# An execution order from a table: attention with a shared key head beside a squared-ReLU layer, on one core

## The chip, the cores and the metric

The program runs on one core of a Trainium2 chip. The time is what the device needs for one execution, in microseconds (us). One execution was taken by the hardware profiler; the views quoted below come from it.

## What is computed

The input x has 2048 rows of 640 values in bfloat16. Each row is normalised to mean 0 and variance 1. The normalised rows go through an attention with 32 query heads of 20 values that share one key and one value head, and through a layer with 1536 hidden values whose activation is the square of a ReLU. Both results are added to x.

```python
xn = (x - mean) / sqrt(var + 1e-5)                     # x: 1 x 2048 x 640
q = heads(xn @ wq)                                     # 32 heads of 20
p = softmax(q @ (xn @ wk).T * 20 ** -0.5)              # one key head for all
a = rows(p @ (xn @ wv)) @ wo
h = relu(xn @ w1 + b1)
out = x + a + (h * h) @ w2 + b2
```

## The kernel before, in words

**Blocks and tiles.** The work of the attention is cut into 32 blocks (`NBLK`): 4 parts of 512 query rows, and for each of them 8 groups of 4 heads. A block has 16 key tiles of 128 keys, and a key tile has 4 score tiles, one for each head: 128 keys by 512 queries. There are 2048 score tiles. A score tile is one product on TensorE (`ps<-qT,kT`) with only 20 rows of the array, so up to four heads can run side by side, each in its own quarter of rows. It lands in one of the eight PSUM banks; bank 7 (`PVB`) holds the sums of the block, the other seven hold scores and the results of all other products.

**Two ways to the exponential.** 1392 of the score tiles go to ScalarE, two in one instruction (L1022, 696 instructions, `make_act`), which writes the exponential to the ring `PT`. The other 656 tiles go to VectorE in 164 sets of four, the four heads of one key tile (`new_set`, `make_dqk`, `after_dqk`). There the exponential is approximated through the bits of a bfloat16: one instruction per tile, D1 (L1234), turns a score into an integer that is read as a bfloat16, which gives a power of two with a straight line inside each binade. Three more copies of the set with a quarter, a half and three quarters of a binade added (the passes P1 to P3) are summed with weights to smooth the line. A pass is an integer addition over 128 x 2048 values. It runs on GpSimd (L1254, as 64-bit integers) or on VectorE (L1256, as 16-bit integers).

**Products with the values.** A key tile from ScalarE gives one group of four products (`make_pv`, `ps<-PT,vx`). A set from VectorE gives up to four such groups, one for each copy (`make_dpv`, `ps<-tmore,vx` and the like). Two copies with the same weight may be summed first, so that TensorE has one group fewer: by a DMA that adds to its destination, issued by GpSimd (L1269), or by VectorE (L1274). Each set has two such pairs, 328 in all.

**Other work.** The projections, the hidden layer and the output products are cut in units of a few groups of products (`Unit`, the list `misc`). VectorE evicts their banks. Each block's sums are normalised through small DMAs on SP's queue (`emit_norm`, L1103 to L1139), which also carries the query rows (L735), the rows of x and the output (L816). Two wide VectorE instructions and the GpSimd passes are marked `lock=True`: the planner never lets two of them run at the same time, and each GpSimd one waits for the last marked VectorE one (`last_lock`). L431 is a helper, `mm`, through which nearly all products are recorded.

**What sets the order.** While the program is built, a planner keeps for each engine the time at which it is free, and takes at each step the candidate that can start first, with priorities from `RULES` that change every 10 us (`consider`, `par`, `commit`). It has a time for each instruction, for instance 0.0631 + 2 x 0.4267 us for an activation (`ACB`, `ACM`), and a margin for each DMA. In this one pass it chooses the order on every engine, the bank of each product, the engine of each pass and the way of each pair. Where TensorE would be idle it may add `fill` products of zeros, so that the busy share stays above a bound (`WARM`). The instructions are then written to five queues in that order, each with waits for what it needs; a queue is worked through in order.

Of the kernel before, what the change touches and what calls it, by code (L numbers as in the profile page):

```python
# [10 lines left out]
I64 = mybir.dt.int64  # L11
# [189 lines left out]

class Ctr:
# [34 lines left out]
class Op:  # L237
    def __init__(self, name, eng, dur, parts, deps=(), lat=None, lock=False, mode="C", prio=3, dma=None):
        self.name, self.eng, self.dur, self.parts = name, eng, dur, parts
        self.deps = [d for d in deps if d is not None]  # L240
        self.lat, self.lock, self.mode, self.prio = lat, lock, mode, prio
        self.dma = dma
        self.start = self.fin = None
        self.consumed = False
        self.tgt = None
        self.clock = None
        self.frees = None
        self.after = None
        self.nb = 0.0
        self.blk = None  # L250
        self.add = False
        self.dw = 0.0
        if dma is not None:
            dma.n += 16
            self.tgt = (dma, dma.n)

    def ready(self):
# [5 lines left out]
        return t  # L263


def bass_parallel_sum__grouped_kv_mqa__dense_activation_squared_relu__prompt_kernel(nc, A_x, A_wq, A_wk, A_wv, A_wo, B_x, B_w1, B_b1, B_w2, B_b2, out):
    es = ExitStack()
    with es:
# [62 lines left out]
        def psbf(bank):  # L331
            return ps[:, bank, :].bitcast(BF16)
# [97 lines left out]
        def mm(out_, l, r, start, stop, tp, loose=False):  # L430
            return lambda e: e.matmul(out_, l, r, start=start, stop=stop, tile_position=tp, skip_group_check=loose)  # L431
# [116 lines left out]
        def col4(lhs, rhs, n, k, last, m=32, bank=None, c0=0, loose=False):  # L548
            bank = ub[0] if bank is None else bank
            return [mm(ps[32 * j:32 * j + m, bank, c0:c0 + n], lhs(j), rhs, k == 0, last, (0, 32 * j), loose) for j in range(4)]  # L550
# [11 lines left out]
        for bk in SHARED:  # L562
            pe_op(f"W{bk}", 0.43, [lambda e, bk=bk: e.matmul(ps[:, bk, :], ones_bf[:, :], hT_tmp[:, 0, :], start=True, stop=True)], [c_ones, c_zero])
# [32 lines left out]
        for st in range(4):  # L596
            bank_rel[st] = q0_op[st]
        q_first = [q0_op[st] for st in range(4)]
# [3 lines left out]
        def fill_parts():  # L602
            return [mm(ps[32 * jj:32 * jj + 32, PVB, :], zeros32[:, :], kT[:, 0:512], False, False, (0, 32 * jj)) for jj in range(4)]
# [40 lines left out]
        def unit_KT(h0, nh):  # L644
# [4 lines left out]
            def evac(p, bk):  # L649
                o = Op(f"KTe{h0}", "DVE", 0.66 if nh == 2 else 0.4, [lambda e: e.tensor_scalar(out=kT[:, cs], in0=ps[:, bk, 0:n], scalar1=nk0[:, 1:2], scalar2=None, op0=ALU.add)],  # L650
# [6 lines left out]
        def unit_V(c):  # L657
            sts = range(4 * c, 4 * c + 4)

            def chunk():  # L660
                r = []
                bk = ub[0]
                for st in sts:
                    for dt in range(DT):
                        r.append(lambda e, st=st, dt=dt: e.matmul(ps[:, bk, DH * (st % 4):DH * (st % 4) + DH], xnT[:, dt, st * 128:(st + 1) * 128], wv_c[:, dt, :],  # L665
# [3 lines left out]
            def evac(p, bk):  # L669
                o = Op(f"Ve{c}", "DVE", 0.16, [lambda e: e.tensor_copy(out=vx[:, 4 * c:4 * c + 4, 0:DH], in_=ps[:, bk, 0:4 * DH].rearrange("p (t d) -> p t d", t=4))],  # L670
# [30 lines left out]
        def unit_QC(qc, c):  # L701
# [4 lines left out]
            def evac(p, bk):  # L706
                k = nqc[0]
                nqc[0] += 1
                o = Op(f"QCe{qc}_{c}", "DVE", 0.60, [lambda e: e.tensor_copy(out=QCr[:, k % NQC, :], in_=ps[:, bk, :])], [p] + qc_dma.get(k - NQC, []))
# [9 lines left out]
        def unit_Q1():  # L719
            ch = [(0.224, (lambda dt=dt: col4(lambda j: wq_sb[:, dt, DH * (HPG + j):DH * (HPG + j) + DH], xnT[:, dt, 0:512], 512, dt, dt == DT - 1, DH))) for dt in range(DT)]  # L720

            def evac(p, bk):
                o = Op("Q1e", "DVE", 0.60, [lambda e: e.tensor_copy(out=qT[:, 1, :], in_=ps[:, bk, :])], [p])
# [23 lines left out]
        def unit_FFN1(qc, f):  # L747
# [4 lines left out]
            def evac(p, bk):  # L752
                k = nffn[0]
                nffn[0] += 1
                o = Op(f"RL{qc}_{f}", "DVE", 0.66, [lambda e: e.tensor_scalar(out=hT_tmp[:, k % 2, :], in0=ps[:, bk, :], scalar1=b1col[:, f:f + 1], scalar2=0.0,  # L755
# [62 lines left out]
        def unit_FP(n):  # L818
# [5 lines left out]
            def evac(p, bk):  # L824
                o = Op(f"FE{n}", "DVE", 0.40, [lambda e: e.tensor_tensor(out=fpw[:, k % NFP, :], in0=ps[:, bk, 0:HW], in1=xrow(st, cs), op=ALU.add)], [p, xr_op[st], fw_op.get(n - NFP)])
# [7 lines left out]
        def unit_OUT(n):  # L833
# [5 lines left out]
            def evac(p, bk):  # L839
                o = Op(f"OE{n}", "DVE", 0.40, [lambda e: e.tensor_tensor(out=out_sb[:, slot, cs], in0=ps[:, bk, 0:HW], in1=xrow(st, cs), op=ALU.add)], [p, xr_op[st], dma_out.get(st - NOS)])  # L840
# [143 lines left out]
        def build_step(j, banks, t0):  # L984
# [3 lines left out]
            banks = banks[:len(tl)]  # L988
            parts, deps = [], []
            for k, (b, kt, h) in enumerate(tl):  # L990
                deps += need_k(kt) + need_q(b)
                deps.append(bank_rel[banks[k]])
                parts.append(mm(ps[:, banks[k], :], kT[32 * h:32 * h + DH, kt * 128:(kt + 1) * 128], qT[32 * h:32 * h + DH, b % NQS, :], True, True, (32 * h, 0)))
            qk = Op(f"QK{j}", "PE", 0.215, parts, deps, mode="R")
            qk.nb = t0
            return dict(j=j, tiles=tl, banks=banks, act=None, nxt=nxt, rest=rest, qk=qk)
# [21 lines left out]
        def make_act(st_):  # L1018
            n, s0, b0 = len(st_["tiles"]), st_["s0"], st_["banks"][0]
            db = st_["banks"][1] - b0 if n > 1 else 1  # L1020
            deps = [st_["qk"]] + [pv_of[t[:2]] for t in st_["old"] if t is not None]
            return Op(f"ACT{st_['j']}", "ACT", ACB + ACM * n, [lambda e: e.activation(out=PT[:, s0:s0 + n, :], in_=ps[:, b0:b0 + (n - 1) * db + 1:db, :], func=AF.Exp, bias=-EXP_SHIFT, scale=SCALE)], deps)  # L1022
# [11 lines left out]
        def make_pv(b, kt):  # L1034
            first, last = b not in pv_begun, pv_count[b] == KT - 1
            parts, deps = [], []
            for h in range(HPG):
                o, sl = tile_act[(b, kt, h)]
                deps.append(o)
                parts.append(mm(ps[32 * h:32 * h + 32, PVB, :], vx[:, kt, :], PT[:, sl, :], first, last, (0, 32 * h)))  # L1040
# [3 lines left out]
            return Op(f"PV{b}_{kt}", "PE", 0.2245, parts, deps)  # L1044

        def make_dpv(s, term):
            b, kt, n = s["b"], s["kt"], s["n"]
            first, last = b not in pv_begun, pv_count[b] == KT - 1 and len(s["terms"]) == 1
            src, wgt = tbuf(s["buf"][term]), (vx if term < 2 else vxs)
            deps = list(s["made"][term])  # L1050
            parts = []
            for h in range(HPG):
                i = s["order"].index(h)
                parts.append(mm(ps[32 * h:32 * h + 32, PVB, :], wgt[:, kt, :], src[:, i * 512:(i + 1) * 512], first, last, (0, 32 * h)))
# [5 lines left out]
            return Op(f"DPV{b}_{kt}_{term}", "PE", 0.2245, parts, deps)  # L1060
# [140 lines left out]
        def make_dqk(heads, what="KEEP"):  # L1201
# [7 lines left out]
            if s is None:  # L1209
# [3 lines left out]
                if s is None:  # L1213
# [6 lines left out]
            return Op(f"DQK{s['n']}_{h}", "PE", 0.215, [mm(ps[:, bank, :], kT[32 * h:32 * h + DH, kt * 128:(kt + 1) * 128], qT[32 * h:32 * h + DH, b % NQS, :], True, True, (32 * h, 0))],  # L1220
                      deps, mode="R"), s, h, bank

        def after_dqk(o, s, h, bank):
# [10 lines left out]
            d1 = op(f"D1_{n}_{i}", "DVE", 0.60, lambda e: e.tensor_scalar(out=L[:, cs].bitcast(U16), in0=ps[:, bank, :], scalar1=XA, scalar2=XB, op0=ALU.mult, op1=ALU.add),  # L1234
                    [o] + (l_users(old) if old else []) + (xr_ if n < NL and s["buf"][0] >= NMORE else []), prio=par("D1P"))
            d1.frees = bank
            d1.blk = s["b"]
# [3 lines left out]
            for j in range(1, NTERM):  # L1241
# [11 lines left out]
                if eng == "POOL":  # L1253
                    fn = lambda e, T=T, j=j: e.int64_add(out=T.bitcast(I64), in0=L.bitcast(I64), in1=TSTEP * j * 0x0001000100010001)  # L1254
                else:
                    fn = lambda e, T=T, j=j: e.tensor_scalar(out=T.bitcast(U16), in0=L.bitcast(U16), scalar1=TSTEP * j, scalar2=None, op0=ALU.add)  # L1256
# [3 lines left out]
                p.blk = s["b"]  # L1260
                s["passes"].append(p)
            for a, (x, y) in ((0, (0, 1)), (3, (3, 2))):
# [33 lines left out]
        def tail_ops():  # L1296
# [16 lines left out]
            for x, bk, p in r:  # L1313
# [4 lines left out]
                yield Op(f"OF{st}_{h}_{c}", "PE", 0.1375, out_chunks(mats, bk, c == 0, c == NCH - 1 or (c == NCH - 2 and k < NPRE), k < NPRE)[0][1](), deps), p, x, bk  # L1318

        def tail_done(o, x, bk):  # L1320
            st, h = x["st"], x["h"]
            if x["c"] == 0:
                x["bank"] = bk
# [4 lines left out]
            if x["c"] == NCH - 1 and k < NPRE:  # L1328
                x["pre"] = op(f"PA{st}_{h}", "DVE", 0.40, lambda e: e.tensor_tensor(out=ps[:, bk, 0:HW], in0=ps[:, bk, 0:HW], in1=part[:, st % 4, cs], op=ALU.add), [o, fr_op[k]], prio=0.25)
# [3 lines left out]
            if x["pre"] is not None:  # L1333
                f_ = op(f"OFe{st}_{h}", "ACT", 0.35, lambda e: e.activation(out=orow(st)[:, cs], in_=ps[:, bk, 0:HW], func=AF.Identity), [o, free_row])
# [349 lines left out]
```

## Time and profile before

| what | us |
|---|---|
| median of 3 runs (lowest to highest) | 665.88 (665.75 to 665.96) |
| profiled execution: its span, the only time of it that the page gives | 666.1 |
| TensorE, products busy | 657.9 |
| ScalarE busy | 650.8 |
| VectorE busy | 605.5 |
| GpSimd busy | 578.3 |

In the profile PE is TensorE, PEld its weight loads, ACT ScalarE, DVE VectorE, POOL GpSimd, SP the queue of most DMAs. An arrow reads "written <- read"; buffer numbers are left out, so `tmore` and `x_sb` stand for all buffers of the sets (`x_sb` is reused for them once x is normalised). A bracket with an arrow at the end of a line gives the idle time before an instruction and what ended it. Instructions overlap at their ends, so a busy share includes some waiting.

### The profile page before, as it was taken

What the parts mean: (1) busy time and instruction counts of PE and PEld (TensorE: products, weight loads), DVE (VectorE), ACT (ScalarE), POOL (GpSimd) and SP (SyncE); (2) the same over time, 40 slices, a digit from 0 to 9 for tenths busy, and PEclk for the clock granted to TensorE, in tenths of its full rate; (3) what the DMA queues carried; (4) which work ended last, traced back from release to release, by engine and by line L of the source; (5) the groups of instructions that cost most, each with busy time, mean ns of one, the idle gap of its engine ahead of it and who ended that gap; (6) DMA issues with size and microseconds to landing.
All of it is one profiled execution on the core that took longest, in us unless ns stands there. A gap on an engine that the chain in (4) does not pass through costs nothing.

```text
span 666.1 us, 22416 instructions
## 1 busy us (share of the span) xinstructions
PE 657.9 (99%) x9593; PEld 209.9 (32%) x9594; DVE 605.5 (91%) x1082; ACT 650.8 (98%) x719; POOL 578.3 (87%) x593
## 2 busy tenths in 40 slices
PE   8999999999999999999999999999999999999998
PEld 4532222332322223333332222333333322223344
DVE  8979999999999999999989999988989999899773
ACT  7999999999999999999999999999999999899995
POOL 1619999999999989999899999999998999899961
PEclk9999999999999999999999999999999999899999
DMA  8897755788877987778788576678788676677873
GB/s 269 253 253 168 163 116 105 157 176 161 176 155 140 192 164 156 152 148 166 143 170 170 119 143 132 133 145 165 139 157 171 142 147 121 128 136 165 168 162 90
DMA packets 54504, 105.23 MB, mean 158 GB/s; under 512 B 16124, under 2 KB 31372, under 8 KB 54340
## 3 DMA queue, kind: packets, MB, share of 16 engines
q0 software_dynamic: 19520, 71.31, 57.5%
q1 hardware_dynamic: 34308, 32.11, 16.7%
q8 instruction: 75, 1.23, 0.7%
q10 hardware_dynamic: 576, 0.38, 0.2%
q14 instruction: 25, 0.20, 0.1%
HBM read 23.26 MB, written 10.01 MB: 50 GB/s over the span
## 4 chain that ended last, share of the span: by engine, by line
PE 85%; POOL 8%; DVE 3%; DMA 2%; issue 1%; ACT 0%; DVEq 0%; POOLq 0%
PE ps L431 84%; POOL tmore L1254 4%; POOL x_sb L1254 3%; DMA tmore<-tmore 1%; DVE tmore L1234 1%; DMA x_sb<-tmore 1%; POOL tmore L1269 1%; PE ps L635 1%; POOL x_sb L1269 0%; PE ps L606 0%; ACT PT L1022 0%; PE ps L665 0%; PE ps L568 0%; DVE OC L1139 0%; DVE ident L445 0%
## 5 line engine op out<-in xcount | busy, mean ns | idle before, releaser
L1022 ACT ACTIVATE PT<-ps 128x1024 bf16<-128x1024 f32 x696 | 641.6, 1073 | 3.9 <-PE ps L431 3.5
L1234 DVE TENSOR_SCALAR tmore<-ps 128x512 uint16<-128x512 f32 x656 | 424.3, 683 | 34.4 <-PE ps L431 25.9
L1254 POOL INT64_ADD tmore<-tmore x219 | 241.9, 1197 | 27.5 <-DVE tmore L1256 11.2
L431 PE MATMUL ps<-qT,kT 20*128 20x512 bf16 x2048 | 264.4, 385 | 1.0 <-DVE tmore L1234 0.6
L1254 POOL INT64_ADD x_sb<-tmore x218 | 241.4, 1228 | 18.9 <-DVE OC L1139 7.3
L431 PEld LDWEIGHTS ps<-qT,kT 20*128 20x128 bf16 x2048 | 66.1, 91 | 256.0 <-ACT PT L1022 226.7
L431 PE MATMUL ps<-PT,vx 128*32 128x512 bf16 x1392 | 132.6, 387 | 0.1
L431 PE MATMUL ps<-xnT,w_sb 128*32 128x512 bf16 x960 | 77.6, 386 | 0.2 <-DVE tmore L1234 0.2
L431 PE MATMUL ps<-w_sb,big 128*32 128x320 bf16 x1536 | 75.3, 302 | 0.1
L1269 POOL DMA_DIRECT2D tmore<-tmore x67 | 69.4, 1047 | 3.0 <-POOL tmore L1254 3.0
L1269 POOL DMA_DIRECT2D x_sb<-tmore x58 | 62.0, 1084 | 3.0 <-POOL x_sb L1254 1.8
L431 PE MATMUL ps<-tmore,vxs 128*32 128x512 bf16 x636 | 57.7, 382 | 0.0
L431 PE MATMUL ps<-x_sb,vxs 128*32 128x512 bf16 x624 | 56.4, 384 | 1.2 <-POOL x_sb L1254 1.2
L431 PEld LDWEIGHTS ps<-PT,vx 128*32 128x32 bf16 x1392 | 33.5, 93 | 62.1 <-issue 55.0
L431 PE MATMUL ps<-tmore,vx 128*32 128x512 bf16 x500 | 47.7, 384 | 0.0
L431 PEld LDWEIGHTS ps<-w_sb,big 128*32 128x32 bf16 x1536 | 33.2, 96 | 28.3 <-issue 18.8
L755 DVE TENSOR_SCALAR hT_tmp<-ps,b1col 128x512 bf16<-128x512 f32 x48 | 35.6, 742 | 0.6 <-PE ps L431 0.5
L431 PE MATMUL ps<-xnT,wq_sb 128*32 128x512 bf16 (+2 forms) x480 | 33.1, 356 | 0.0
L431 PE MATMUL ps<-x_sb,vx 128*32 128x512 bf16 x328 | 32.2, 382 | 0.3 <-DMA x_sb<-tmore 0.3
L431 PE MATMUL ps<-wo_c,OC 128*32 128x320 bf16 x576 | 29.7, 301 | 0.0
L431 PEld LDWEIGHTS ps<-xnT,w_sb 128*32 128x32 bf16 x960 | 18.6, 95 | 27.4 <-issue 21.1
L840 DVE TENSOR_TENSOR out_sb<-ps,xr 128x320 bf16<-128x320 f32 x24 | 11.7, 487 | 11.0 <-PE ps L431 11.0
(98 smaller groups left out, 330.0 us busy)
## 6 DMA issues: line engine op xcount, KB each, us to landing
tmore<-tmore POOLq DMA_DIRECT2D x67, 512.0 KB, 5.7
x_sb<-tmore POOLq DMA_DIRECT2D x58, 512.0 KB, 5.4
w_sb<-in_B_w_dram SPq DMA_DIRECT2D x8, 480.0 KB, 11.9
big<-OR SPq DMA_DIRECT2D x71, 40.0 KB
xb<-in_A_x_dram SPq DMA_DIRECT2D x1, 2560.0 KB, 13.1
xb<-b2r POOLq DMA_DIRECT2D x1, 2560.0 KB, 19.5
xr<-xb SPq DMA_DIRECT2D x16, 160.0 KB, 4.3
out_dram<-out_sb SPq DMA_DIRECT2D x15, 160.0 KB, 2.8
```

The costliest lines, as they stand in the source:

```text
L431: return lambda e: e.matmul(out_, l, r, start=start, stop=stop, tile_position=tp, skip_group_check=loose)
L635: return [(lambda e, dt=dt: e.transpose(out=psbf(bk)[:, dt * 128:(dt + 1) * 128], in_=xn_sb[:, st, dt:D:DT], identity=ident[:])) for dt in ...
L755: o = Op(f"RL{qc}_{f}", "DVE", 0.66, [lambda e: e.tensor_scalar(out=hT_tmp[:, k % 2, :], in0=ps[:, bk, :], scalar1=b1col[:, f:f + 1], scal ...
L840: o = Op(f"OE{n}", "DVE", 0.40, [lambda e: e.tensor_tensor(out=out_sb[:, slot, cs], in0=ps[:, bk, 0:HW], in1=xrow(st, cs), op=ALU.add)], [ ...
L1022: return Op(f"ACT{st_['j']}", "ACT", ACB + ACM * n, [lambda e: e.activation(out=PT[:, s0:s0 + n, :], in_=ps[:, b0:b0 + (n - 1) * db + 1:db ...
L1234: d1 = op(f"D1_{n}_{i}", "DVE", 0.60, lambda e: e.tensor_scalar(out=L[:, cs].bitcast(U16), in0=ps[:, bank, :], scalar1=XA, scalar2=XB, op0 ...
L1254: fn = lambda e, T=T, j=j: e.int64_add(out=T.bitcast(I64), in0=L.bitcast(I64), in1=TSTEP * j * 0x0001000100010001)
L1269: p = op(f"AD{a}_{n}", "POOL", ADDUR, lambda e, src=src, dst=dst: e.dma_start(dst, src, accum_op=ALU.add), dp + [ad_last.get(k)], dma=adse ...
```

## The change

The planner runs as before and still decides which tiles go to ScalarE, in which order, and which to VectorE. What it plans for TensorE, VectorE, GpSimd and SP is then only the start of a second step:

- For each pass both forms, GpSimd's and VectorE's, are made, and for each pair all three ways (product by product, DMA sum, VectorE sum). The table `PLAN["on"]` has five digits for each of the 164 sets: for the three passes 0 is GpSimd and 1 VectorE; for the two pairs 0 is no sum, 1 a DMA, 2 VectorE.
- `PLAN["PE"]`, `["DVE"]`, `["POOL"]`, `["SP"]` reorder each of those queues. An entry k takes the k-th of the instructions that are still left, counted from 0, so a row of zeros keeps the order. There is no table for ScalarE.
- `PLAN["held"]` names for 302 of the 843 GpSimd candidates the VectorE instruction that it waits for; the replay adds the last marked one where it isn't among them.
- `replay` runs the four queues and ScalarE's with fixed durations (`RC`) and chooses the banks: a product takes, of the free banks, the one that is ready first. Banks are objects (`Ref`) whose number is filled in there. Which product of a block starts and which ends its sum follows from the replayed order. Fill products that would lie outside an open sum are left out.
- Waits that other waits already imply are left out by a new search (`needs`).

```diff
+class Ref:
+    def __init__(self, n):
+        self.n = n
...
+def unpack(text, n):
+    left, r = list(range(n)), []
+    for k in repeats(text):
+        r.append(left.pop(int(k)))
+    return r + left
...
+RC = dict(SAME=0.0027, CR=0.105, RC=0.098, FIRST=0.010, LANE=0.004, ACT=0.9035, ACTPE=0.2215, POOLP=1.008, AD=0.915, QK=0.425, DVEPE=0.155, STOP=114, STOPT=1.2)
...
+def replay(seq, pool, order_all):
...
+            if e == "PE":
+                if o.mode != mode:
+                    t += RC["CR"] if mode == "C" else RC["RC"]
+                elif o.mode == "R":
+                    t = max([held["t"] + RC["LANE"] * len(held["o"].lanes)] + [lane[h] for h in o.lanes])
...
+            if o.lock:
+                t = max(t, lock)
+                if e == "POOL" and lastlock is not None:
+                    t = max(t, fin[lastlock] + LATS["DVE", "POOL"])
...
+        if o.lock and e == "POOL" and lastlock is not None and lastlock not in o.deps:
+            o.deps.append(lastlock)
...
+            d = o.dur
+            if e == "ACT" and o.name[:3] == "ACT":
+                d = RC["ACT"]
+            if e == "POOL":
+                if o.add:
+                    d = RC["AD"]
...
+            if o.add:
+                b = max(t + ADLEAD, dma)
+                dma = b + ADGAP
+                land[o] = b + ADLAND
...
+PLAN = {
+    "PE": (
+        "0*176 1 0*2 4 2 1 0*2 1 0 1*2 2 1 2 4 3 2*2 8 3 2 6 1 0 3 2*2 1 2 1*3 3 2*3 3 2 0 5 4 3 1 2 3*2 2*2 1 0 2 1*2 0 2 1 0*2 3 2 1*2 3 2*2 1 5 4 3 1 8 1 3 2 1 2 3 2*3 0 2 1 2 "
...
+    "held": (
+        "-*2 31*2 50 56*11 - 95 103*2 116 118 -*4 141 130*2 155 - 155*2 -*2 141 -*2 155 -*2 155 -*2 175 - 188 -*4 186 -*5 203 - 216*2 188 -*3 231*3 -*2 216 -*3 216 - 216 -*5 258 "
...
+    "on": (
+        "11000000000000100000000101000000010000100011000000000100001000000000000000010010000100010000010000100001000010000000101000010001101001000100100100001000010011101100000010"
...
+        "00010000100001000000000100001000010001000000000010001100000000000001000001000110000100001000000100100100001010000100110211122111101110211122"),
+}
...
-        for o in order_all:
-            for d in o.deps:
-                if not (o.eng == "PE" and d.eng == "PE"):
-                    d.consumed = True
...
+        for s in sets:
+            n = s["n"]
+            for j in range(1, NTERM):
+                p = s["orig"][j][0]
+                q = Op(p.name, "DVE" if p.eng == "POOL" else "POOL", PPASS if p.eng == "DVE" else 0.60, [p.fns["DVE" if p.eng == "POOL" else "POOL"]],
+                       [d for d in p.deps if d is not lib_op and d is not p.held] + ([lib_op] if p.eng == "DVE" else []), lock=True)
+                choice([p, q] if p.eng == "POOL" else [q, p], p)
...
+        for e in ENG:
+            if e in PLAN:
+                old = seq[e]
+                seq[e] = [old[k] for k in unpack(PLAN[e], len(old))]
+        if "on" in PLAN:
+            for g, c in zip(groups, PLAN["on"]):
+                for k, o in enumerate(g):
+                    o.on = k == int(c)
...
+        fins = replay(seq, pool, order_all)
...
+            if o.name == "fill" and o.tail and not open_:
+                continue
```

More of the change, by code (lines that the diff above doesn't have):

```diff
@@ L252, in __init__ @@
         self.dw = 0.0
+        self.tail, self.on, self.also = False, True, []
+        self.takes, self.gives, self.lanes, self.brel, self.chain, self.ends, self.sums, self.held = [], [], [], [], None, None, None, None
         if dma is not None:
@@ L988, in build_step @@
             banks = banks[:len(tl)]
+            refs = [Ref(bk) for bk in banks]
             parts, deps = [], []
```

357 lines of the change are left out of this document (297 added, 60 removed), and 82 rows, old and new, of the table PLAN.

## The prediction

> **What bounds the kernel now.** I read the page's busy shares first, then the timeline of ScalarE, then the chain of waits around each place where ScalarE stood still.
>
> ```profile
> span 666.1 us, 22416 instructions
> PE 657.9 (99%) x9593; PEld 209.9 (32%) x9594; DVE 605.5 (91%) x1082; ACT 650.8 (98%) x719; POOL 578.3 (87%) x593
> ```
>
> Every engine looks full, so the shares decide nothing. The timeline of ScalarE does (start, length, what, how many; in brackets the idle time before). The first two rows are two windows that begin with the same activation; the other five are the whole kernel.
>
> ```profile
> 369.94 20.36 ACT L1022 ACTIVATE PT<-ps 128x1024 bf16<-128x1024 f32 x22
> ...
> 369.94 70.78 ACT L1022 ACTIVATE PT<-ps 128x1024 bf16<-128x1024 f32 x77
> ...
> 12.26 148.97 ACT L1022 ACTIVATE PT<-ps 128x1024 bf16<-128x1024 f32 x161 [0.24 <-PE ps L431]
> 161.44 333.61 ACT L1022 ACTIVATE PT<-ps 128x1024 bf16<-128x1024 f32 x362 [0.21 <-PE ps L431]
> 495.85 71.87 ACT L1022 ACTIVATE PT<-ps 128x1024 bf16<-128x1024 f32 x78 [0.80 <-PE ps L431]
> 569.10 1.02 ACT L1022 ACTIVATE PT<-ps 128x1024 bf16<-128x1024 f32 x1 [1.39 <-PE ps L431]
> 571.04 86.48 ACT L1022 ACTIVATE PT<-ps 128x1024 bf16<-128x1024 f32 x94 [0.92 <-PE ps L431]
> ```
>
> From the first two rows, 55 activations end (70.78 - 20.36) / 55 = 0.9167 us apart where nothing disturbs them, and one alone takes 1.02. All 696 at that pace would take 1.02 + 695 x 0.9167 = 638.1 us; begun at 12.26 they would end at 650.4. They end at 571.04 + 86.48 = 657.5. So ScalarE sets the time and loses **7.1 us**: 0.21 + 0.80 + 1.39 + 0.92 = 3.3 us in four gaps, all ended by TensorE, and 3.8 us in delays too short to empty it. After its last exponential come 666.1 - 657.5 = 8.6 us of tail. No reordering can give more than these 7.1 us and a part of the tail.
>
> Why TensorE was late is in the chain of waits (start, length, what), the DMA issues and one look at TensorE:
>
> ```profile
> 153.69 6.95 DMA x_sb<-tmore
> ...
> 485.71 8.03 DMA tmore<-tmore
> ...
> 541.36 2.36 POOL tmore L1254 x2
> ...
> 561.13 3.11 POOL x_sb L1254 x3
> 564.24 1.25 issue
> ...
> tmore<-tmore POOLq DMA_DIRECT2D x67, 512.0 KB, 5.7
> x_sb<-tmore POOLq DMA_DIRECT2D x58, 512.0 KB, 5.4
> ...
> 567.51 0.58 PE L431 MATMUL ps<-x_sb,vxs 128*32 128x512 bf16 x4 [1.08 <-POOL x_sb L1254]
> ...
> 564.00:567.50 3.50, 2.43 (x33) 1.00 0.50 95
> 567.50:571.00 3.50, 3.48 (x30) 0.52 0.71 147
> ```
>
> The gaps at 161 and 495 follow pair sums by DMA that landed 6.95 and 8.03 us after their issue, where the median is 5.4 to 5.7. The two near 570 follow a run of GpSimd passes that chain back to 541: TensorE stood 1.08 us for one, was busy 2.43 of 3.50 us, and in the next 3.5 us had a granted clock of 0.52. One late GpSimd pass thus cost ScalarE 1.39 + 0.92 = 2.3 us. The Trainium skill (TensorE: Matmul & The Clock Gate, Part 1) has the clock halve after an idle window of about 3.4 us. The trace agrees on the half and on its length, but here 1.08 us of standing was enough; by the figure of the Trainium skill this gap would have cost only the standing.
>
> **The change part by part.** I counted the table of choices (five digits to each of 164 sets of four score tiles): 90 passes on VectorE and 402 on GpSimd; 122 pair sums by DMA, 6 on VectorE, 200 pairs not summed. Before:
>
> ```profile
> L1254 POOL INT64_ADD tmore<-tmore x219 | 241.9, 1197 | 27.5 <-DVE tmore L1256 11.2
> L1254 POOL INT64_ADD x_sb<-tmore x218 | 241.4, 1228 | 18.9 <-DVE OC L1139 7.3
> ...
> L1269 POOL DMA_DIRECT2D tmore<-tmore x67 | 69.4, 1047 | 3.0 <-POOL tmore L1254 3.0
> L1269 POOL DMA_DIRECT2D x_sb<-tmore x58 | 62.0, 1084 | 3.0 <-POOL x_sb L1254 1.8
> ...
> L1256 DVE TENSOR_SCALAR tmore<-tmore 128x2048 uint16<-128x2048 uint16 x28 | 21.5, 772 | 0.1
> L1256 DVE TENSOR_SCALAR x_sb<-tmore 128x2048 uint16<-128x2048 uint16 x27 | 21.2, 790 | 0.1
> ...
> L1269 POOL DMA_DIRECT2D x_sb<-x_sb x4 | 4.2, 1060 | 0.0
> L1269 POOL DMA_DIRECT2D tmore<-x_sb x2 | 1.9, 958 | 0.3 <-POOL x_sb L1254 0.3
> L1274 DVE TENSOR_TENSOR tmore<-tmore 128x2048 bf16<-128x2048 bf16 x1 | 2.1, 2062 | 0.7 <-POOL tmore L1254 0.7
> ...
> 486.54 0.40 PE L431 MATMUL ps<-x_sb,vx 128*32 128x512 bf16 x4
> 486.76 0.39 PE L431 MATMUL ps<-x_sb,vxs 128*32 128x512 bf16 x4
> ```
>
> GpSimd loses 437 - 402 = 35 passes of (241.9 + 241.4) / 437 = 1.11 us and 131 - 122 = 9 issues of some 1.05: 38.9 + 9.5 = **48 us less** of its 578. VectorE gains 35 passes of 42.7 / 55 = 0.78 us, 27 us, and three sums of at most 2.1 us (the longest of three), 6 us. TensorE gains six product groups, 0.22 us apart in the last two rows: 1.3 us. ScalarE's order isn't in the table; its 696 activations stay.
>
> What hides the VectorE work: the last four sets have twelve of the 90 passes and five of the six sums, so up to 9.4 + 10.5 us, some of it done earlier, lie where VectorE has 13.9 us free. The other 78 - 55 = 23 passes, 17.9 us, lie in the middle:
>
> ```profile
> 66.60:632.80 566.20, 563.51 (x7926) 167.37 (x7918) 526.54 (x882) 562.84 (x612) 533.60 (x539) 1.00 0.75 151
> 632.80:666.10 33.30, 30.20 (x663) 15.87 (x659) 19.38 (x34) 26.41 (x31) 12.55 (x13) 1.00 0.53 126
> ...
> 563.62 1.18 DVE L1256 TENSOR_SCALAR tmore<-tmore 128x2048 uint16<-128x2048 uint16 x1
> ```
>
> The third busy time is VectorE's: 526.5 + 17.9 = 544.4 of 566.2. Bounds: a pass can take 1.18, as in the last row, where three GpSimd passes ran until 564.24 (row 561.13) and it ended at 564.80; 23 x 1.18 = 27.1 still fits. If that cover were gone, the price is the 18 to 27 us themselves; I take nothing. The Trainium skill (SBUF - State Buffer, "SBUF: two separate sides") says that such a VectorE instruction and a GpSimd one exclude each other for the whole instruction, the loser fully blocked. The row of 1.18 agrees with it, and by that rule every moved pass stays at the dear end of its bounds.
>
> The added waits of GpSimd on VectorE: the planner before gives each GpSimd pass a wait for the last such VectorE instruction too, and the table and the replay only say which. Queued behind a waiting pass stand the next passes and sums, and TensorE waits for those; the row of L1254 has 11.2 us of it in all, mostly once, and the 48 us freed on GpSimd cover it. I take nothing, with one stop like that at 567.5, 2.3 us, as the upper end.
>
> TensorE's order and the banks: 2203 of 3336 entries take something other than the next in line, yet a mean of 2.7 places away. Nothing in the trace prices this. Lower end: all 3.8 us of small delays go. Upper end: three stops like the one at 567.5, 6.9 us. I take half of the small delays, 1.9 us, because the row x77 shows that stretches without any exist.
>
> SP's queue is moved most (mean 6.9 places of 499), and it works in order:
>
> ```profile
> SPq L1105 <- DVE OR L1103: 70.9, 17, 10.1
> ```
>
> It already stands up to 10.1 us at a row's normalisation, with loads of qT and output rows behind. The margins of the plan stay, so I take nothing; the upper end is one stop of that length, 10.1 us.
>
> The tail: after the last transpose come the final products of eight half rows.
>
> ```profile
> 659.73 0.71 DVE L1101 STREAM_TRANSPOSE QCr<-QCr 128x512 bf16<-128x512 bf16 x1
> ...
> 660.50 0.46 PE L431 MATMUL ps<-w_sb,QCr 128*32 128x320 bf16 x8
> ...
> 662.82 0.31 PE L431 MATMUL ps<-w_sb,QCr 128*32 128x320 bf16 x4
> ```
>
> These are the first and last of twelve rows with 72 matmuls; 32 read QCr and had to wait, 40 did not. 40 / 72 of the 662.82 + 0.14 - 660.50 = 2.5 us is 1.4 us that an order could bring forward, if banks were free. I take 0.7; nothing to 1.4 are the ends (and below nothing, if VectorE's work of the last four sets is late: the row 632.80 leaves little).
>
> **The sum**, on the profiled execution's 666.1: gaps, 3.3 less a remainder of 0.7, because GpSimd and the sums by DMA lose work exactly there: -2.6. Small delays -1.9. Tail -0.7. The six product groups lie in the waits before score matmuls. 666.1 - 5.2 = 660.9. The page gives the execution no time but its span, and the median of the three runs is 0.2 lower: **660.7 us**. What is late next is ScalarE itself, at its own pace.
>
> **The rivals.** *The gaps only move.* They came from single late landings and late passes, and another order meets others: 665.9, within 0.2%. For it: 122 sums remain, and 8.03 against 5.7 shows how landings scatter, while the replay in the diff has one constant for them. Against: GpSimd has 48 us less to do, and the replay's ScalarE takes 0.9035 us where the rows show 0.9167, so the others run with 1.4% more room than it was laid out for.
>
> *The clock falls more often (slower).* The replay gives matmuls one duration whatever the clock. Where a tight order lets TensorE stand about 1 us in 3.5, it runs at half clock for 3.5 us and ScalarE loses 2.3, as at 567.5. The place is any product group whose pass or sum was ordered close behind its maker. On top of 660.7, one gives 663.0, two 665.3, and **from three** it is slower: 667.6. By the figure of the Trainium skill cited above a stop would cost only its 1.1 us of standing, and six would be needed. For the rival: such a stop happened once in an order that put fill products into gaps by rule, and the replay has no such rule of its own. Against: GpSimd's and DMA's lightened load.
>
> *The table moves little*, since each queue's entries shift by two to seven places: then only the lightened GpSimd works, 666.1 - 2.6 - 0.2 = 663.3, still faster.
>
> **How the numbers follow.** Forecast 0.50; little moved 0.17; gaps move 0.15; clock falls 0.18. The low end is all 7.1 and 1.4 gone: 657.4. The high end takes in the slower case at its threshold: 668.0. What a measurement tells from no change is about 0.2%, 1.3 us: the forecast and the third rival are faster (0.67), the first is the same (0.15), the clock is slower (0.18).
>
> **What would show it.** Right: ScalarE's rows in two or three long pieces, its last exponential near 653, 402 and 90 passes, no stretch below clock 1.00 after the start. Wrong: gaps ended by TensorE with a granted clock near 0.5 behind them, VectorE above 98% in a middle stretch with score matmuls waiting for its evictions, or a tail over 8.6 us.

## The result, and the profile after

The changed kernel is slower: 668.85 us (median of 4 runs, 668.23 to 669.29) against 665.82 (4 runs, 665.24 to 665.96), a ratio of 1.0046 with a 95% interval of 1.0032 to 1.0060. The forecast was 660.7 and its range ended at 668.0. Measured again in experiment nine it took 667.79, ratio 1.0032 (1.0019 to 1.0045).

The run that was profiled took 669.29; its page has

```profile
span 667.5 us, 22412 instructions
PE 659.2 (99%) x9618; PEld 213.7 (32%) x9618; DVE 623.0 (93%) x1120; ACT 650.2 (97%) x719; POOL 538.9 (81%) x549
...
PE 89%; DMA 6%; POOL 3%; DVE 1%; issue 0%; ACT 0%
...
L1517 POOL INT64_ADD tmore<-tmore x200 | 216.0, 1119 | 36.4 <-DVE big L1008 17.4
L1517 POOL INT64_ADD x_sb<-tmore x202 | 219.7, 1117 | 20.0 <-DVE big L1008 6.2
...
L1518 DVE TENSOR_SCALAR tmore<-tmore 128x2048 uint16<-128x2048 uint16 x47 | 32.8, 708 | 1.4 <-PE ps L675 1.3
...
L1518 DVE TENSOR_SCALAR x_sb<-tmore 128x2048 uint16<-128x2048 uint16 x43 | 29.4, 692 | 0.0
...
tmore<-tmore POOLq DMA_DIRECT2D x63, 512.0 KB, 5.7
x_sb<-tmore POOLq DMA_DIRECT2D x54, 512.0 KB, 5.7
```

The change did what it says: 402 passes on GpSimd and 90 on VectorE, GpSimd 39 us less busy, VectorE 17.5 us more. GpSimd's new stops behind VectorE are in its rows (56 us idle in the two groups, 46 before), and the chain of the third line shows next to nothing of VectorE. But the sums by DMA land no sooner: a median of 5.7 us in both groups, 5.7 and 5.4 before.

The timeline of ScalarE, as it was read for the kernel before (start, length, what, how many; in brackets the idle time before):

```profile
12.19 17.20 ACT L1274 ACTIVATE PT<-ps 128x1024 bf16<-128x1024 f32 x18 [0.24 <-PE ps L675]
29.87 2.85 ACT L1274 ACTIVATE PT<-ps 128x1024 bf16<-128x1024 f32 x3 [0.48 <-PE ps L675]
33.58 49.92 ACT L1274 ACTIVATE PT<-ps 128x1024 bf16<-128x1024 f32 x54 [0.85 <-PE ps L675]
83.80 55.10 ACT L1274 ACTIVATE PT<-ps 128x1024 bf16<-128x1024 f32 x60 [0.30 <-PE ps L675]
139.07 28.58 ACT L1274 ACTIVATE PT<-ps 128x1024 bf16<-128x1024 f32 x31 [0.17 <-PE ps L675]
168.53 95.54 ACT L1274 ACTIVATE PT<-ps 128x1024 bf16<-128x1024 f32 x104 [0.88 <-PE ps L675]
264.30 94.60 ACT L1274 ACTIVATE PT<-ps 128x1024 bf16<-128x1024 f32 x103 [0.22 <-PE ps L675]
359.89 139.35 ACT L1274 ACTIVATE PT<-ps 128x1024 bf16<-128x1024 f32 x151 [0.99 <-PE ps L675]
499.44 51.53 ACT L1274 ACTIVATE PT<-ps 128x1024 bf16<-128x1024 f32 x56 [0.20 <-PE ps L675]
551.41 39.87 ACT L1274 ACTIVATE PT<-ps 128x1024 bf16<-128x1024 f32 x43 [0.45 <-PE ps L675]
591.45 24.86 ACT L1274 ACTIVATE PT<-ps 128x1024 bf16<-128x1024 f32 x27 [0.17 <-PE ps L675]
616.52 42.30 ACT L1274 ACTIVATE PT<-ps 128x1024 bf16<-128x1024 f32 x46 [0.22 <-PE ps L675]
```

By the prediction's own account ScalarE now loses 616.52 + 42.30 - 12.19 - 638.1 = 8.5 us, 7.1 before: 4.9 in eleven gaps where there were 3.3 in four, and 3.6 in delays that don't empty it. TensorE ends every gap. They are of three kinds.

**Late sums.** In the chain of waits five steps are sums by DMA (start, length):

```profile
160.32 7.27 DMA tmore<-tmore
...
351.31 7.75 DMA x_sb<-x_sb
...
471.28 6.85 DMA x_sb<-tmore
...
542.95 7.63 DMA x_sb<-tmore
...
607.75 7.54 DMA x_sb<-tmore
```

Each lands some 0.8 to 1.2 us before the end of one of the gaps at 168, 360, 551 and 617, or before a smaller delay at 479. TensorE stands at the product group that reads it (0.23 to 0.97 us), at two of them so:

```profile
167.63 0.40 PE L675 MATMUL ps<-tmore,vx 128*32 128x512 bf16 x4 [0.64 <-DMA tmore<-tmore]
...
359.10 0.40 PE L675 MATMUL ps<-x_sb,vxs 128*32 128x512 bf16 x4 [0.97 <-DMA x_sb<-x_sb]
```

**The lead.** Before, the score group near 29.6 us ran whole; after, it is in two halves, and the second waits until ScalarE has freed a bank. The row of before:

```profile
29.57 0.40 PE L431 MATMUL ps<-qT,kT 20*128 20x512 bf16 x4
```

and the rows of after:

```profile
30.09 0.39 PE L675 MATMUL ps<-qT,kT 20*128 20x512 bf16 x2
30.95 0.39 PE L675 MATMUL ps<-qT,kT 20*128 20x512 bf16 x2 [0.48 <-ACT PT L1274]
```

TensorE's table begins with 176 zeros, which is the planner's order up to some 45 us, so what differs here is the bank that the replay chose. The gaps of 0.48 and 0.85 us follow. That the bank is the cause is tested in experiments one, two and five.

**Gaps without a wait** (84, 139, 264, 499, 591; 1.06 us): TensorE doesn't stand over 0.1 us in the 6 us before them; other products come ahead of the score group.

### The profile page after: what moved, and what is told of

Its sections match the earlier page's. It is cut to its first block, busy times and chain, and to the rows that moved or that the text cites. A ratio compares the mean times of both kernels' runs of the same rounds, so it can differ in the third digit from the quotient of the medians.

```text
span 667.5 us, 22412 instructions
## 1 busy us (share of the span) xinstructions
PE 659.2 (99%) x9618; PEld 213.7 (32%) x9618; DVE 623.0 (93%) x1120; ACT 650.2 (97%) x719; POOL 538.9 (81%) x549
## 4 chain that ended last, share of the span: by engine, by line
PE 89%; DMA 6%; POOL 3%; DVE 1%; issue 0%; ACT 0%
PE ps L675 88%; DMA x_sb<-tmore 3%; POOL tmore L1517 1%; DMA x_sb<-x_sb 1%; DMA tmore<-tmore 1%; POOL x_sb L1517 1%; PE ps L880 1%; PE ps L851 0%; POOL tmore L1534 0%; PE ps L910 0%; PE ps L812 0%; DVE tmore L1497 0%; DVE OR L752 0%; ACT PT L1274 0%; DVE ident L689 0%
## 5 line engine op out<-in xcount | busy, mean ns | idle before, releaser
L1517 POOL INT64_ADD tmore<-tmore x200 | 216.0, 1119 | 36.4 <-DVE big L1008 17.4
L1517 POOL INT64_ADD x_sb<-tmore x202 | 219.7, 1117 | 20.0 <-DVE big L1008 6.2
L675 PE MATMUL ps<-w_sb,big 128*32 128x320 bf16 x1536 | 80.0, 302 | 0.0
L1534 POOL DMA_DIRECT2D tmore<-tmore x63 | 63.3, 1004 | 9.1 <-DVE tmore L1518 4.7
L675 PE MATMUL ps<-x_sb,vxs 128*32 128x512 bf16 x624 | 59.5, 383 | 1.0 <-DMA x_sb<-x_sb 1.0
L675 PE MATMUL ps<-tmore,vxs 128*32 128x512 bf16 x632 | 60.4, 383 | 0.0
L1534 POOL DMA_DIRECT2D x_sb<-tmore x54 | 52.4, 970 | 5.3 <-POOL x_sb L1517 3.0
L675 PE MATMUL ps<-tmore,vx 128*32 128x512 bf16 x528 | 50.8, 384 | 0.6 <-DMA tmore<-tmore 0.6
L1518 DVE TENSOR_SCALAR tmore<-tmore 128x2048 uint16<-128x2048 uint16 x47 | 32.8, 708 | 1.4 <-PE ps L675 1.3
L1518 DVE TENSOR_SCALAR x_sb<-tmore 128x2048 uint16<-128x2048 uint16 x43 | 29.4, 692 | 0.0
```

The lines of the kernel that those rows point to most:

```text
L675: return lambda e: e.matmul(out_(), l, r, start=val(start), stop=val(stop), tile_position=tp, skip_group_check=loose)
L1517: fns = dict(POOL=lambda e, T=T, j=j: e.int64_add(out=T.bitcast(I64), in0=L.bitcast(I64), in1=TSTEP * j * 0x0001000100010001), DVE=lambda ...
L1518: DVE=lambda e, T=T, j=j: e.tensor_scalar(out=T.bitcast(U16), in0=L.bitcast(U16), scalar1=TSTEP * j, scalar2=None, op0=ALU.add))
L1534: p = op(f"AD{a}_{n}", "POOL", ADDUR, lambda e, src=src, dst=dst: e.dma_start(dst, src, accum_op=ALU.add), dp + [ad_last.get(k)], dma=adse ...
```

## The experiments

My theory was that two things cost: sums that land later than the replay's constant, and the replay's bank choice in the lead. A third suspicion was that before's profile had shown more to win than a usual run has. The rivals: the replay's machinery costs by itself; or the gaps only move. The expectations count with each gap the 0.1 us by which an activation after a gap takes longer (1.02 against 0.9167): their 0.59 and 0.96 us are the 0.48 and 0.85 above.

### The kernel before, once more (four)

> The kernel before, profiled once more. Theory (the stretch of half clock at 567 us belonged to that one execution, so the 2.3 us that I meant to win there are not in the usual time): span about 664.0, run time 1.8 above it, clock 1.00 in all stretches after the start, and no gaps of ScalarE near 570. Rival (it is in every execution): span 666 and the same half clock at 567.

Measured: span 664.6, time 666.47. Its timeline of ScalarE, and TensorE at the late GpSimd pass:

```profile
12.26 11.29 ACT L1022 ACTIVATE PT<-ps 128x1024 bf16<-128x1024 f32 x12 [0.24 <-PE ps L431]
23.78 3.91 ACT L1022 ACTIVATE PT<-ps 128x1024 bf16<-128x1024 f32 x4 [0.23 <-PE ps L431]
27.94 467.36 ACT L1022 ACTIVATE PT<-ps 128x1024 bf16<-128x1024 f32 x507 [0.24 <-PE ps L431]
495.91 71.86 ACT L1022 ACTIVATE PT<-ps 128x1024 bf16<-128x1024 f32 x78 [0.61 <-PE ps L431]
568.55 87.55 ACT L1022 ACTIVATE PT<-ps 128x1024 bf16<-128x1024 f32 x95 [0.78 <-PE ps L431]
```

```profile
567.57 0.40 PE L431 MATMUL ps<-x_sb,vxs 128*32 128x512 bf16 x4 [1.08 <-POOL x_sb L1254]
```

```profile
564.00:567.50 3.50, 2.48 (x33) 0.55 (x25) 3.50 (x6) 3.50 (x5) 2.24 (x4) 1.00 0.51 99
567.50:571.00 3.50, 3.43 (x47) 0.95 (x47) 2.75 (x5) 2.66 (x4) 3.50 (x5) 1.00 0.74 153
```

The stop of 1.08 us is there again, with TensorE busy 2.48 of 3.50 us; the half clock is not. The expectation was right on the clock and wrong on the gap, of which 0.78 us stay. So the stop belongs to the kernel and the half clock only to some of its executions: the cores' view gives the first profile of before a mean clock of 0.997, and of 88 runs of the kernel before, taken beside the first eleven experiments, nine had 0.997 (their median is 667.6 us; where in them the clock fell isn't known). In this profile, whose time is near the median, ScalarE loses 568.55 + 87.55 - 12.26 - 638.1 = 5.7 us, not 7.1. A run's time is some 1.8 us above its span in every list of runs (666.06 and 664.2, for one), so the profiled execution took about 667.9, where the median is 666. I had set its span beside the median and not seen that it was a slow one.

### No table, with the replay's banks (one) and the planner's (five)

```diff
+PLAN = {}
```

Five has in `replay` as well:

```diff
...
+                if o.start < 1e9:
+                    can = {k: v for k, v in can.items() if k in [x.n for x in o.takes]}
...
```

> The changed kernel with an empty table: the order, the pass engines and the pair sums are the planner's again, while the banks are still given out by the replay and the GpSimd passes still wait as the replay says. Theory 1 (the table's order lets five product groups wait for pair sums by DMA that land later than the replay's constant, 3.2 us, and the replay's bank choice delays the lead, 1.4 us): the late sums of the table go and the planner's own two or three come back (0.2 and 0.8 us at 161 and 495), the bank choice stays: 666.5 to 667.5, with the gaps at 30 and 33 us still there. Rival (the replay's machinery costs by itself, its waits or its banks, whatever the order): 668.5 or more. Rival (the table's order is worth what I forecast and the machinery takes more away): over 670.

> The changed kernel with an empty table, as in the first experiment, and now with the banks that the planner names as well; what is left of the change is that the replay says when GpSimd passes wait for VectorE. Theory (of the 0.9 us that the empty table still cost, all is the two gaps near 30 and 33 us, which are the banks): as the kernel before, 665.8 to 666.5, and those gaps gone. Rival (the new waits of GpSimd, or code that the change adds, cost by themselves): 667.1, the gaps gone but delays elsewhere.

Measured: 667.08, ratio 1.0020 (1.0010 to 1.0030), with the gaps of 0.48 and 0.85 us at 30 and 34; with the planner's banks 665.71, ratio 0.9993 (0.9984 to 1.0003), without them. The machinery costs nothing that these runs could tell; its bank choice costs 1.4 us, by the ratios 1.8. Experiment one lies within its theory's range, five 0.1 us under it.

### The table with the planner's banks in the lead (two)

The products planned before 42 us take the planner's banks, later ones those of the changed kernel (the list `BANKS`, and in `replay` the lines that keep to `want`, are left out here).

```diff
...
+        takers = [o for o in seq["PE"] if o.takes]
+        digits = iter(BANKS)
+        for o in takers:
+            o.want = [int(next(digits)) for _ in o.takes]
+            if o.start < 42:
+                o.want = [x.n for x in o.takes]
```

> The changed kernel with the banks that the planner names for every product planned before 42 us, and the banks of the changed kernel's own run after that; the table stays. Theory 1: the gaps of 0.59 and 0.96 us near 29.9 and 33.6 us go, since the order of TensorE is the planner's there and only the banks differ: about 1.4 us less, 667.4. Rival (what the lead gains is lost again at the next wait for a pair sum by DMA, which lands at its own time): 668.8, with a longer gap at 168.

Measured: 666.85, ratio 1.0012 (1.0001 to 1.0022). The score group is whole again:

```profile
29.50 0.40 PE L680 MATMUL ps<-qT,kT 20*128 20x512 bf16 x4
```

ScalarE's first gap is now at 45.65 us, 0.33, where the two bank choices meet. It gained 2.0 us, more than the 1.4 expected; beside experiment nine, by the ratios, 1.3. The lead's banks are shown, with the table and without it; they are the larger part of the loss. With them mended the table is still no gain.

### Readers of late sums, further back (three and six)

```diff
+        for n, y in [(30, 1), (82, 2), (115, 1), (136, 1), (153, 1)]:
+            q, o = seq["PE"], sets[n]["pv"][y]
+            k = q.index(o)
+            q.remove(o)
+            q.insert(k + 8, o)
```

That is experiment three, with the changed kernel's own banks held fixed. Six leaves out (30, 1), moves the others by 4, and has the lead's banks of two.

> The changed kernel with its own banks fixed and the five product groups that waited for late pair sums (ScalarE gaps 0.99, 1.10, 0.20, 0.55, 0.33 us) each put eight places further back in TensorE's queue. Theory 1 (only the scatter of the landings against a constant in the replay costs): the five gaps go, 3.2 us less: 665.7; a part may come back where other groups now stand close behind their sums: up to 667. Rival (TensorE is short of time there and any order pays the same): 668.8, with gaps of the same sum at other places.

> The second experiment's banks for the lead, and four of the five groups of the third experiment put four places further back in TensorE's queue (sets 82, 115, 136 and 153); the one of set 30 stays where the table has it, because a buffer of VectorE's first pass waits behind it. Theory (a sum by DMA lands late at the same place in every execution, so moving its reader is a lasting gain; the third experiment lost it only at set 30): the gaps of 0.72 and 0.43 us of the second experiment near 358 and 549 go: 665.7, at or below the kernel before. Rival (what the readers gain is lost to the groups that take their places): 666.9, as the second experiment.

Measured: three 668.52, ratio 1.0038 (1.0026 to 1.0051); six 666.98, ratio 1.0020 (1.0007 to 1.0034), as the second. Both fall to the rival. Six's own profile is of the fastest of its runs and loses 588.30 + 67.36 - 12.18 - 638.1 = 5.4 us, less than the 5.7 of before; the median shows no gain. Where the loss goes in three (VectorE, TensorE and ScalarE in turn):

```profile
167.60 0.69 DVE L1502 TENSOR_SCALAR tmore<-ps 128x512 uint16<-128x512 f32 x1 [0.56 <-DMA tmore<-tmore]
...
168.35 0.39 PE L680 MATMUL ps<-qT,kT 20*128 20x512 bf16 x3 [0.65 <-DVE tmore L1502]
...
171.01 0.39 PE L680 MATMUL ps<-qT,kT 20*128 20x512 bf16 x3 [0.99 <-DVE tmore L1502]
...
171.48 1.02 ACT L1279 ACTIVATE PT<-ps 128x1024 bf16<-128x1024 f32 x1 [1.66 <-PE ps L680]
```

VectorE's D1 of a later set writes into the buffer that the late sum and its readers still hold. It waits for the DMA, its bank stays taken, and TensorE's next scores wait for the bank, 0.65 us and, behind the next D1, 0.99: 0.88 us of gap became 1.66. The gaps at 360 and 551 did go; the profile still loses 8.2 us in all (8.5 before the edit). The reader was not the only one behind the sum.

### Orders fitted to measured landings (seven and eight), and the change again (nine)

Sum by sum the landings of two profiles of this table correlate at 0.83 to 0.93 and differ by 0.3 to 0.5 us (root mean square). So a search moved TensorE's products, from the order of six, with each sum's mean landing from three profiles in place of the constant.

```diff
+MOVED = "..."
+        seq["PE"] = [seq["PE"][k] for k in unpack(MOVED, len(seq["PE"]))]
```

> The second experiment's banks for the lead, and TensorE's order put through a search that gives each of the 122 pair sums by DMA the landing that the profiles of the changed kernel and of experiments two and three measured for it (they agree with each other sum by sum) in place of one constant, and each exponential 0.9167 us; 366 to 439 places of TensorE's 3336 change. Theory (what is left after the lead is TensorE standing behind sums whose landing the table was laid out without): about 2 us less than the second experiment, 664.5 to 665.3, below the kernel before. Rival (landings vary from run to run as much as from sum to sum, so an order fitted to some profiles meets other delays): 666.5 to 667.5.

> The same search begun from another seed, so another order with the same aim. Theory: 664.5 to 665.5, with the seventh kernel; rival: 666.5 to 667.5; if the two lie apart by over 1 us, it is the single order that counts and not the landings.

> The changed kernel unaltered, on the same chip as the two others, so that the lead banks and the rest are compared with it directly. Both theories: 668.5 to 669.2, gaps near 30 and 33 us as before; landings late at the same sums as in its first profile.

Measured: 667.13, ratio 1.0018 (1.0006 to 1.0030), and 667.10, 1.0022 (1.0009 to 1.0035): no better than the second. Nine: 667.79 (667.46 to 668.88), lower than expected. Its first profile was the slowest of its runs and the second the fastest (span 665.7), as the rival would have it. From 139 us on, the second has

```profile
139.07 124.19 ACT L1274 ACTIVATE PT<-ps 128x1024 bf16<-128x1024 f32 x135 [0.16 <-PE ps L675]
263.48 94.61 ACT L1274 ACTIVATE PT<-ps 128x1024 bf16<-128x1024 f32 x103 [0.22 <-PE ps L675]
358.90 139.44 ACT L1274 ACTIVATE PT<-ps 128x1024 bf16<-128x1024 f32 x151 [0.82 <-PE ps L675]
498.54 91.28 ACT L1274 ACTIVATE PT<-ps 128x1024 bf16<-128x1024 f32 x99 [0.20 <-PE ps L675]
589.98 67.02 ACT L1274 ACTIVATE PT<-ps 128x1024 bf16<-128x1024 f32 x73 [0.16 <-PE ps L675]
```

The lead's two gaps and the gaps without a wait are the same to 0.01 us; of the gaps at late sums only the one at 359 is left. ScalarE loses 589.98 + 67.02 - 12.18 - 638.1 = 6.7 us, 1.8 less, and 1.7 of that in the gaps at late sums, with the program unaltered. Whether both profiles come from one chip isn't on record. The median landing is 5.5 and 5.4 us in its DMA issues.

### One and two readers of the order before (ten and eleven)

The same edit as in three, on kernel five: `(142, 3)` by six places, the reader of the late pass at 567.57; in eleven `(30, 1)` by two as well.

> The empty table with the planner's banks (the fifth experiment, as fast as the kernel before), and one product group of TensorE, the one that waited 1.09 us for a GpSimd pass at 567.57 in it, put six places further back in TensorE's queue. Theory (this late pass is late in every execution, because GpSimd stands 1.26 us at the same DMA issue each time, and nothing else waits on the reader): the gap near 569 goes, 0.9 to 1.1 us, and with it the half clock that sometimes follows: 664.7, below the kernel before. Rival (as with the readers of DMA sums, the gain is lost to what stands behind): 665.7 to 666.1.

> As the tenth, and the reader of the pair sum of set 30, at which ScalarE lost 0 to 0.5 us near 161 in the profiles of the planner's order, two places further back. Theory (its sum lands late by about the same each time): a further 0.1 to 0.4 us: 664.4. Rival (its landing differs from run to run, so that it pays in some and costs in others): the same as the tenth within 0.3.

Measured: 666.40, ratio 1.0001 (0.9992 to 1.0009); 667.32, ratio 1.0020 (1.0006 to 1.0034). The rival again. In ten the stop of 1.08 us is gone, and 3 to 5 us later stand

```profile
570.50 0.40 PE L680 MATMUL ps<-xnT,w_sb 128*32 128x512 bf16 x4 [0.19 <-DVE tmore L1502]
...
572.61 1.02 ACT L1279 ACTIVATE PT<-ps 128x1024 bf16<-128x1024 f32 x1 [0.32 <-PE ps L680]
```

Summed over the activations that end between 566 and 578 us, each end less the end before and the pace of 0.9167, ScalarE loses 1.1 us in ten, 1.5 in kernel five and 1.15 in the second profile of before. Of the 1.10 us that kernel five lost at 569, most came back 3 to 8 us later, and the times show no gain. Nor did the half clock go: ten has a run with a mean clock of 0.997, and eleven three with 0.997 or 0.995, so a part of eleven's 667.32 is half clock.

### Less work for TensorE (twelve to fourteen)

```diff
-col4(..., r, 320, kk, ...)
+col4(..., r if kk == 0 or k == n - 1 else r[:, 0:80], 320 if kk == 0 or k == n - 1 else 80, kk, ...)
```

> The changed kernel, in which the middle steps of the output products (all but the first and last of each sum) work on 80 of 320 columns, so part of the output is left out; every order, bank and wait is that of the changed kernel. Some 450 groups of four matmuls lose about 0.1 us each, 45 us of TensorE's 659. Theory (TensorE's load is the cause of the gaps without a wait, 2.2 us near 83, 139, 264, 378, 440, 499, 577 and 591): these go, the two gaps of the lead stay: about 2 us below the changed kernel, 665.6 to 666.5. Rival (orders and waits are the cause): 667.5 to 668.8, gaps as they were.

> The second experiment (table, lead's banks mended) with the same part of the output products left out. Theory: 664.3 to 665.0, ScalarE's gaps only at late sums by DMA and at the seam of the two bank choices near 45 us. Rival: 666.5 to 667.

> The fifth experiment (empty table, the planner's banks) with the same part of the output products left out. Theory (TensorE's load also makes the small delays of the planner's order, 2.3 us): 663.5 to 664.5, so that the table is worth nothing even with TensorE relieved. Rival (waits): 665.3 to 666.2.

Measured: 706.68, 699.91 and 699.10, ratios 1.0524 (1.0485 to 1.0562), 1.0485 (1.0449 to 1.0521) and 1.0485 (1.0451 to 1.0520): by the ratios, 31 to 33 us more than the kernels that they were made from. Both theories fall, and the granted clock with them: in fourteen its mean is 0.924. With 440 groups shortened, windows of fourteen read (length, busy of PE, PEld, DVE, ACT, POOL, then clock):

```profile
127.00:131.00 4.00, 3.42 (x67) 1.01 (x65) 3.55 (x7) 4.00 (x5) 4.00 (x5) 0.85 0.93 191
131.00:134.50 3.50, 3.50 (x37) 0.70 (x33) 3.02 (x4) 2.80 (x4) 2.51 (x4) 0.69 0.53 103
```

and TensorE in the first of them

```profile
127.55 0.39 PE L680 MATMUL ps<-qT,kT 20*128 20x512 bf16 x3 [0.27 <-ACT PT L1279]
...
130.66 0.61 PE L680 MATMUL ps<-qT,kT 20*128 20x512 bf16 x4
```

TensorE does its work and stands for ScalarE, 0.3 us at a time, ScalarE full beside it. Behind 0.58 us of such standing in 4 its products take 0.61 us instead of 0.39. The same window of kernel five has TensorE busy 4.00 of 4.00 at clock 1.00. But standing isn't what the falls of the clock have in common. In thirteen the clock falls where the profile shows none (the same columns):

```profile
257.77:261.18 3.41, 3.41 (x60) 1.26 (x58) 3.32 (x7) 3.41 (x5) 2.45 (x3) 1.00 0.59 116
261.19:264.60 3.41, 3.41 (x33) 0.72 (x32) 2.19 (x5) 2.83 (x3) 2.66 (x3) 0.50 0.78 149
```

After the start, the clock records of these traces change only in steps of 3.41 us. Counted from the instructions of thirteen and fourteen, with a product on a quarter of the array as a quarter, 20 of 22 falls between 12 us and the last 40 follow a step in which products of at most 3552 columns in all were begun; of 306 other steps at full clock 8 had so few, and the middle one has 5632. So the falls go with little work in a step, which shorter products give even without standing. That is a correlation; no run tests apart what in such a step makes the clock fall. Whether the gaps without a wait come from TensorE's load these runs can't say.

## Why the prediction was wrong

- **That ScalarE sets the time at 0.9167 us a piece** held: the 60 activations of after's row at 83.80 end (55.10 - 1.02) / 59 = 0.9166 us apart.
- **The starting point** was off: some 1.4 of the 7.1 us belonged to a half clock that, by the mean clock, nine of 88 runs show. Set on the usual run, the same reductions would have given less: some 1.4 us of the -2.6 for gaps were not there to be had. The sum also mixed two scales: 660.9 is a span, and the time that goes with it is some 1.8 us more, 662.7, where I took 0.2 off. From the span forecast, 660.9, to the one measured, 667.5, the rest is gaps (4.9 for 0.7), small delays (3.6 for 1.9) and the tail (8.7 for 7.9).
- **"Gaps, -2.6, because GpSimd and the sums by DMA lose work exactly there"** is the step that failed. GpSimd did lose the work; the landings didn't change (5.7 us), and the table put other readers close behind them. In two profiles its gaps came to 4.9 and 3.2 us (late sums 2.5 and 0.8, the lead 1.3, the rest without a wait), where 0.7 had been forecast, against 1.9 in the usual profile of before (0.23 + 0.24 + 0.61 + 0.78). The rival "the gaps only move" described this: with the lead mended the kernel was at 1.0012, within its 0.2%, and six attempts to take gaps away (three, six, seven, eight, ten, eleven) gave nothing or lost.
- **"TensorE's order and the banks: nothing in the trace prices this. Small delays -1.9"** failed as well, and turned the sign. The small delays went from 3.8 (5.7 - 1.9) to 3.6 and 3.5 us (8.5 - 4.9, 6.7 - 3.2). The banks cost 1.33 us in two gaps at the start, 1.4 to 2.0 by the medians. It lay inside the upper end of 6.9, but as a clock event; I looked for a late pass and not for a bank. A replay that chooses banks greedily had to be followed through the first 35 us, where the table's zeros leave TensorE's order alone.
- **The other rivals.** "The table moves little", 663.3, missed for the same reason as the forecast: it kept the -2.6. The clock falling more often didn't happen: the core's clock is 1.000 in all nine runs of the changed kernel. Its price of 2.3 us a stop was read from one execution: in experiment four the same kernel has the same stop without the half clock, and ScalarE loses 1.05 us at it. Slower came by another mechanism than the one I had priced.
- **VectorE's passes cost nothing** on the path, as I took. They were cheaper than forecast: 62.2 us for 90, 0.69 each, against 0.78. By the section "SBUF: two separate sides" of the Trainium skill (SBUF - State Buffer) a moved pass might have stayed at the dear end, near 1.18. These runs can't test that: by the timeline after, a pass of VectorE lies beside one of GpSimd for at most 0.25 us, where the pass of 1.18 did so for 0.62.
- **The added waits of GpSimd, nothing**: held as far as tested (kernel five has the replay's waits and the time of before; the chain of after has 1% of VectorE). With the table's own waits alone it wasn't tried. **SP, nothing**: no step of the chain is SP's.
- **The tail, -0.7**: nothing. It is 667.5 - 658.8 = 8.7 us. The final products still wait for the last transposed rows:

```profile
662.09 0.32 PE L675 MATMUL ps<-w_sb,QCr 128*32 128x320 bf16 x4
...
664.41 0.31 PE L675 MATMUL ps<-w_sb,QCr 128*32 128x320 bf16 x4
```

From the first to the last that reads QCr it is 2.32 us, as before (660.50 to 662.82).

**What stays open.** The rest, 0.1% (0.01 to 0.22%) with the lead mended, lies between the gaps without a wait (about 1 us; past the first 30 us the usual profile of before has none) and the late sums, which differ by 1.7 us between the two profiles of the changed kernel. I couldn't part them, and no version beat the kernel before.

## What to carry to other kernels

Profile the kernel twice before pricing what a gap is worth, set the profiled execution's own time and clock beside the median, and count only gaps that come back. A late result holds more than its reader: before moving the reader, see who waits for its buffer and its bank, or the gap only moves. An order laid out against fixed landings meets their scatter, here some 0.4 us a sum from one profile to the next and over 1 us at single sums; and where a table leaves the order alone but a greedy allocator chooses anew, follow the allocator.

## What the hardware showed that was not expected

- TensorE's clock halves without an idle window, and standing doesn't tell when. The stop of 1.08 us halved it in one profile of before and not in the other, though TensorE was busy 2.33 of the step's 3.41 us in both (564.19 to 567.60, 564.91 to 568.32); in thirteen it fell behind 3.41 of 3.41. The Trainium skill (TensorE: Matmul & The Clock Gate, Part 1) gives an idle window of about 3.4 us and calls the window free-running. The runs agree with the window's length, and disagree with the need for a whole idle window: none of these was one. The same page ("A second HAM failure mode: psum-queue depth-cycling") tells of a clock that swings when TensorE stands briefly between groups again and again; experiment fourteen shows such a swing, thirteen one in part without standing that the profile shows.
- So taking away some 40 us of TensorE's work (the 440 groups went from 0.20 to some 0.11 us each, by the rows of five and fourteen) made the kernel 31 to 33 us slower, with nothing else altered.
- Sums by DMA of 512 KB land in the same pattern each time, but not at the same time. The one at 160.32 took 7.27 us in the first profile after and 6.04 in the second; its reader, which stood 0.64 us in the first, has no wait in the second:

```profile
166.77 0.39 PE L675 MATMUL ps<-tmore,vx 128*32 128x512 bf16 x4
```
